# A four-layer attention kernel: one constant scale for all weights, and a first chunk in float16 parts

## Chip, core and metric

The kernel runs on one core of a Trainium2 chip. The metric is device time in microseconds (us) of one execution; lower is better. TensorE (PE) multiplies matrices, ScalarE (ACT) evaluates functions, VectorE (DVE) and GpSimd (POOL) do elementwise work, and SyncE (SP) issues the transfers (DMA) between the memory of the device (DRAM) and the memory beside the engines (SBUF). TensorE writes into PSUM, from which ScalarE and VectorE read.

## The reference

Four layers, windowed and full attention in turn, each with a layer norm before it and a residual addition behind it. S = 2048 rows, D = 512, H = 32 heads of 16, a window of 256 keys. Layers 0 and 2 use the A weights, layers 1 and 3 the B weights.

```python
def _A_ref(x, wqkv, wo):
    qkv = (x @ wqkv).reshape(B, S, 3, H, Dh).transpose(2, 0, 3, 1, 4)
    q, k, v = qkv[0], qkv[1], qkv[2]
    scores = jnp.einsum("bhqd,bhkd->bhqk", q, k) * (Dh ** -0.5)
    mask = (idx[:, None] - idx[None, :] >= 0) & (idx[:, None] - idx[None, :] < W)
    scores = jnp.where(mask[None, None], scores, -1e9)
    o = jnp.einsum("bhqk,bhkd->bhqd", softmax(scores), v)
    return o.transpose(0, 2, 1, 3).reshape(B, S, D) @ wo
# _B_ref: the same without the mask
x = x + _A_ref(_layernorm(x), A_wqkv, A_wo)
x = x + _B_ref(_layernorm(x), B_wqkv, B_wo)
x = x + _A_ref(_layernorm(x), A_wqkv, A_wo)
x = x + _B_ref(_layernorm(x), B_wqkv, B_wo)
```

The weights are drawn as 0.05 times standard normal numbers.

## The kernel before

**Tiling.** The rows are worked on in four chunks of 512 (`QC`, index `c`), the heads in eight groups of four (`qd`). `layers` and `mats` name eight weight matrices of 512 x 512, `(ty, s)`: `ty` is the kind of layer (0 windowed, 1 full), `s` is 0 for queries, 1 for keys, 2 for values, 3 for the output projection. For each chunk of a layer the kernel projects keys (`keys`, name `K`), queries (`queries`, `Q`) and values (`values`, `VV`), runs attention over the heads, and applies the output projection with the residual addition and the statistics of the next layer norm (`wo`, `OO`; in the last layer `wo_part`, `O3`, for a quarter of the heads at a time).

**Numbers in two float16 parts.** Activations and weights are split into a high part (the number rounded to float16) and a low part (what is left of it). A product is the sum of three matmuls, high by high, high by low and low by high (`TERMS`, line 439), so a projected tile of 128 x 512 takes 12 matmuls (four slices of the contraction). `mms` (line 419) emits them; in the full layers each is issued as four of 32 columns, one by one among the attention's matmuls.

**Scales.** So that the split holds for weights of any size, each column of a matrix is divided by a power of two near its largest magnitude. `maxima` (line 284) reduces the magnitudes on DVE and turns the result with four TensorE transposes; `scales` (line 312) cuts out the exponent, spreads it over the partitions with a product of a diagonal matrix and ones (`dg`, `ug`, L327), and puts the results in `wd`, `gcol` and `es`; `parts` (line 339) multiplies the matrix (`mul`, L344), casts it (ScalarE, L345) and subtracts (`rest`, L346), and writes the split matrix to DRAM (`wd`). `share` divides the exponents of queries and keys between both. What was divided out comes back where a result leaves PSUM: `es` in `project` (L525, L527, L528), `gcol` in `wo` and `wo_part` (L652, L673), each followed by an addition to x.

**The first chunk** is different. Its projections start before any scale is known, from unsplit float32 weights and a float32 copy `xT` of the normalized chunk, with four float32 matmuls a tile; the maxima are taken meanwhile (`first_maxima`), and the factors are applied when the tile leaves PSUM. The A matrices of queries, keys and values are split behind that (`parts(..., True)`) and stay in SBUF (`WT`) for the second chunk; all later users load them from DRAM (`weights`, line 391, L397 and L399). The other five matrices are prepared during the first layer's attention (`prep`, work `PR`).

**Order.** TensorE's order is written by hand: a planner with its own clock (`clock`, `spent`, `wait`) mixes "side" works (class `Work`: projections, output projections, preparations) with the attention's steps, three a group in the windowed layers and 16 a group in the full ones (`side0` to `side3` list them by chunk). A work marked `aside` costs TensorE little and is stepped on whenever its time has come. The instructions of all other engines, and SP's transfers, are put in order by a list scheduler from the program order, their dependencies and an estimate of durations; each engine then runs its own list strictly in order. A tile's `bufs` says how many buffers rotate under its tag: a load into a tag waits until the oldest buffer is free.

**Attention.** In the full layers a step is two pairs of score matmuls (L714), two exponentials of 128 x 1024 on ScalarE (L718) and four products with the values (L758); the side works there have one PSUM bank (`acc[1]`), which DVE empties. In the windowed layers POOL cuts the window out of the exponentials (L781, L784) before the products (L791). `epilogue` (line 678) turns the accumulated result on DVE (L686), divides it and splits it (`oh`, L701, L702).

The last lines compare the smallest and the sum of the softmax denominators with bounds and set `flag`; if it isn't good, `general_path` computes everything again.

Of the kernel before, what the change touches and what calls it, by code (L numbers as in the profile page):

```python
# [13 lines left out]
I32 = mybir.dt.int32  # L14
# [21 lines left out]
L_SUM = 2.0 ** 60  # L36

# [149 lines left out]
def fast_path(ctx, tc, flag, a_x, a_wqkv, a_wo, b_wqkv, b_wo, out):  # L187
# [21 lines left out]
    CM, DN, DC, WT, ST, pend = {}, {}, {}, {}, {}, []  # L209
# [16 lines left out]
    perm = cp.tile([P, P], F32, name="perm")  # L226
    onesf = cp.tile([P, P], F32, name="onesf")
    ones = cp.tile([P, QC], F16, name="ones")
    hsum = cp.tile([P, 32], BF16, name="hsum")
    es = cp.tile([P, 2, 2, NHT], F32, name="es")  # L230
    upv = cp.tile([P, 2, NHT], F32, name="upv")
    gcol = [cp.tile([P, D], F32, name=f"gcol{i}") for i in range(2)]
    zeros = cp.tile([P, QC], F16, name="zeros")
    lmin = cp.tile([P, QC // 32], F32, name="lmin")
    lsum = cp.tile([P, QC // 32], F32, name="lsum")

# [8 lines left out]
    nc.gpsimd.tensor_copy(perm.rearrange("p (h u d) -> p u h d", u=2, d=DH), ident.rearrange("p (u h d) -> p u h d", u=2, d=DH))  # L245
# [12 lines left out]
    nc.vector.memset(lsum, 0.0)  # L258

# [24 lines left out]
    def maxima(ty, s, raw):  # L284

        n = f"{ty}_{s}"
        if s == 3:
            for k in range(NC):
                nc.vector.tensor_scalar(raw[:, k, :], raw[:, k, :], upv[:, ty, k:k + 1], None, op0=ALU.mult)
        cm = CM[ty, s] = vp.tile([P, NHT], F32, name=f"wc{n}", tag="wc", bufs=8)  # L290
        am = vp.tile([P, D], F32, name=f"wa{n}", tag="dn", bufs=2)
        for h in range(4):
            f = slice(h * P, (h + 1) * P)
            nc.vector.tensor_reduce(am[:, f], raw[:, :, f].rearrange("p k f -> p f k"), axis=AX.X, op=ALU.max,
                                    apply_absolute_value=True)
            yield
        pt = bank().rearrange("p (t f) -> p t f", f=P)
        for t in range(NHT):
            nc.tensor.transpose(pt[:, t, :], am[:, t * P:(t + 1) * P], ident)
        nc.vector.tensor_reduce(cm, pt, axis=AX.X, op=ALU.max)  # L300

    def first_maxima(s, raw, tiles):

        if (0, s) not in CM:
            CM[0, s] = vp.tile([P, NHT], F32, name=f"wc0_{s}", tag="wc", bufs=8)
        for t in tiles:
            pt = bank()
            for k in range(NC):
                nc.tensor.transpose(pt[:, k * P:(k + 1) * P], raw[:, k, t * P:(t + 1) * P], ident)
            nc.vector.tensor_reduce(CM[0, s][:, t:t + 1], pt, axis=AX.X, op=ALU.max, apply_absolute_value=True)  # L310

    def scales(ty, s):

        n = f"{ty}_{s}"
        cm = CM.pop((ty, s))
        up = es[:, ty, s, :] if s < 2 else vp.tile([P, NHT], F32, name=f"wu{n}", tag="wc", bufs=8)
        dn = vp.tile([P, NHT], F32, name=f"wn{n}", tag="wc", bufs=8)
        nc.vector.tensor_scalar(up.bitcast(I32), cm.bitcast(I32), 0x7F800000, None, op0=ALU.bitwise_and)
        nc.vector.tensor_scalar(dn.bitcast(I32), up.bitcast(I32), -1, 0x7F000000, op0=ALU.mult, op1=ALU.add)
        DC[ty, s] = dn  # L320
        for v, name in ((up, "u"), (dn, "d"))[0 if s == 3 else 1:]:
            dg = vp.tile([P, NHT, P], F32, name=f"{name}g{n}", tag="oe")
            nc.vector.tensor_tensor(dg, ident[:, None, :].broadcast_to([P, NHT, P]),
                                    v[:, :, None].broadcast_to([P, NHT, P]), ALU.mult)
            yield
            pb = bank()
            nc.tensor.matmul(pb, onesf, dg.rearrange("p t f -> p (t f)"), start=True, stop=True)  # L327
            if name == "u":
                nc.vector.tensor_copy(gcol[ty], pb)
            else:  # L330
                DN[ty, s] = vp.tile([P, D], F32, name=f"wd{n}", tag="dn", bufs=2)
                nc.scalar.activation(DN[ty, s], pb, AF.Copy)
        if s == 2:

            pu = bank()
            nc.tensor.matmul(pu[:, :NHT], perm, up, start=True, stop=True)
            nc.vector.tensor_copy(upv[:, ty, :], pu[:, :NHT])

    def parts(ty, s, raw, act):

        dnb = DN.pop((ty, s))
        w = wp.tile([P, NC, 2, D], F16, name=f"w{ty}_{s}", tag="vf", bufs=NQ)
        hi, lo = w[:, :, 0, :], w[:, :, 1, :]
        mul = lambda k: (nc.vector if act else nc.gpsimd).tensor_tensor(raw[:, k, :], raw[:, k, :], dnb, ALU.mult)  # L344
        cast = lambda k: nc.scalar.activation(hi[:, k, :], raw[:, k, :], AF.Copy)  # L345
        rest = lambda k: nc.gpsimd.tensor_tensor(lo[:, k, :], raw[:, k, :], hi[:, k, :], ALU.subtract)  # L346
        if act:
            for k in range(NC):
                mul(k), cast(k), rest(k)
                yield  # L350
            WT[ty, s] = w
        else:

            for f, n, pause in (mul, 1, 2), (cast, 2, 1), (rest, 1, 0):
                for k in range(NC):
                    f(k)
                    if k % n == n - 1:
                        yield
                for _ in range(pause):
                    yield  # L360
        nc.sync.dma_start(wd[ty, s], w)

    def prep(ty, s):
        raw = load_w(ty, s)
        yield wait(14)
        for _ in maxima(ty, s, raw):
            yield wait(2)
        yield -spent(1.0)
        for _ in scales(ty, s):
            yield wait(4)  # L370
        if (ty, s) == (1, 0):
            share(1)
        yield -spent(0.5)
        for _ in parts(ty, s, raw, False):
            yield wait(2)

    def share(ty):

        s = vp.tile([P, NHT], F32, name=f"sh{ty}", tag="sh")
        h = vp.tile([P, NHT], F32, name=f"sg{ty}", tag="sh")  # L380
        q, k = (es[:, ty, i, :].bitcast(I32) for i in (0, 1))
        s, h = s.bitcast(I32), h.bitcast(I32)
        nc.vector.tensor_scalar(s, q, 1, None, op0=ALU.logical_shift_right)
        nc.vector.tensor_scalar(h, k, 1, None, op0=ALU.logical_shift_right)
        nc.vector.tensor_tensor(s, s, h, ALU.add)
        nc.vector.tensor_scalar(k, s, 0x7F800000, None, op0=ALU.bitwise_and)
        nc.vector.tensor_tensor(s, s, k, ALU.subtract)
        nc.vector.tensor_tensor(h, s, s, ALU.add)
        nc.vector.tensor_tensor(q, k, h, ALU.add)
# [103 lines left out]
    def transpose(l, c, xns):  # L493
        for i, xh in enumerate(xns):
            yield "wait", XNR[l, c] + 2.3 * i
            transposed(l, c, i, xh)

    def project(l, s, c, act, ht=None, first=None):


        ty, n = l % 2, f"{l}_{s}_{c}" + ("" if ht is None else f"_h{ht}")
# [540 lines left out]
    def all_of(works, following=()):  # L1042
        Side(1, works, following).finish()
# [151 lines left out]
```

## Time and profile before

| what | us |
| --- | --- |
| median of three runs | 2763.53 (2763.45 to 2769.7) |
| span of the profiled execution | 2769.2 |
| busy: PE | 2639.3 |
| busy: ACT | 2376.7 |
| busy: DVE | 961.8 |
| busy: POOL | 567.1 |
| first score matmul of the first layer (L714) | at 63.78 |

A row of the profile names line, engine and operation, then output and inputs by the program's names with their shapes and a count. Groups give busy time, the mean duration of one in ns, and the idle time of the engine ahead of them with what ended it. In an order-of-time view the first number is the start and the second the length; a bracket at the end is idle time ahead of the row and what ended it. "PEld" is the loading of TensorE's stationary operand, which overlaps matmuls. The chain and the waits are inferred from semaphores, and the ends of matmuls are modelled. Times are from one execution.

### The profile page before, as it was taken

The page shows a single profiled execution, that of the slowest core. Times are in us where ns is not written, and L with a number is a line of the kernel's source. Part 1 is how long each engine was busy: PE and PEld are TensorE (multiplying, and loading weights), DVE is VectorE, ACT ScalarE, POOL GpSimd, SP SyncE. Part 2 cuts the span into 40 slices and gives each one's busy share as a digit, 9 for nine tenths or more (in the row PEclk, how much of TensorE's full clock was granted, in tenths as well). Part 3 has the DMA queues.
Part 4 walks back from the last instruction along what each step waited for, and adds up shares of the span by engine and source line. Part 5 has one row for each costly group of instructions (what it writes and reads, how often), then busy time and mean ns, then how long its engine had stood idle before and what let it go on. Part 6 is the DMA issues. An engine that isn't in the chain of part 4 may idle for free.

```text
span 2769.2 us, 59663 instructions
## 1 busy us (share of the span) xinstructions
PE 2639.3 (95%) x24358; PEld 782.1 (28%) x24358; DVE 961.8 (35%) x2059; ACT 2376.7 (86%) x2687; POOL 567.1 (20%) x1129
## 2 busy tenths in 40 slices
PE   8989989999999999999998899899999999999997
PEld 4333334322222222222223333522222222222221
DVE  7678765112131113112215576512222222222122
ACT  3566655799999999999995667399999999999997
POOL 2477662000000000000004677200000000000000
PEclk9999999999999999999999999999999999999999
DMA  6877775422232123212325474613333343333331
GB/s 218 224 251 221 221 208 153 143 74 86 84 100 91 60 85 107 85 60 91 99 71 170 146 195 126 187 59 108 104 118 116 118 124 105 102 107 115 98 94 56
DMA packets 317501, 344.78 MB, mean 125 GB/s; under 512 B 113056, under 2 KB 233376, under 8 KB 311200
## 3 DMA queue, kind: packets, MB, share of 16 engines
q1 hardware_dynamic: 317216, 340.86, 40.3%
q8 instruction: 193, 3.16, 0.5%
q14 instruction: 92, 0.75, 0.1%
HBM read 228.07 MB, written 96.99 MB: 117 GB/s over the span
## 4 chain that ended last, share of the span: by engine, by line
PE 73%; ACT 9%; DVE 6%; issue 5%; POOL 3%; DMA 2%; SPq 0%; ACTq 0%; DVEq 0%; POOLq 0%
PE acc L758 30%; PE s L714 19%; PE b L432 10%; PE acc L429 10%; ACT e L718 8%; PE acc L791 3%; PE bs L432 1%; POOL e L781 1%; POOL e L784 1%; DVE ot L686 1%; POOL wr L344 1%; DVE sp L528 1%; DVE xh L469 0%; DVE xn L463 0%; DVE xh L463 0%
## 5 line engine op out<-in xcount | busy, mean ns | idle before, releaser
L718 ACT ACTIVATE e<-s 128x1024 f32<-128x1024 f32 (+2 forms) x2432 | 2243.3, 1116 | 99.4 <-PE s L714 89.4
L758 PE MATMUL acc<-e,vt 128*17 128x512 f32 x8192 | 1077.9, 598 | 5.3 <-DVE ot L686 4.1
L714 PE MATMUL s<-qt,kt 64*128 64x512 f16 (+3 forms) x5504 | 780.1, 355 | 64.7 <-ACT e L718 40.2
L714 PEld LDWEIGHTS <-kt 64*128 64x128 f16 x5504 | 204.6, 94 | 816.5 <-issue 789.8
L784 POOL TENSOR_SCALAR_AFFINE_SELECT e<-e 128x256 f32<-128x256 f32 x512 | 230.1, 457 | 119.2 <-ACT e L718 118.2
L758 PEld LDWEIGHTS acc<-e,vt 128*17 128x17 f32 x8192 | 136.2, 95 | 379.5 <-issue 347.9
L686 DVE STREAM_TRANSPOSE ot<-acc 128x512 f32<-128x512 f32 x128 | 91.3, 713 | 381.8 <-PE acc L758 317.3
L781 POOL TENSOR_SCALAR_AFFINE_SELECT e<-e 128x256 f32<-128x256 f32 x448 | 199.0, 451 | 92.2 <-ACT e L718 89.9
L702 POOL TENSOR_TENSOR oh<-o,oh 128x512 f16<-128x512 f32 x31 | 36.0, 1161 | 884.6 <-DVE oh L701 884.6
L791 PE MATMUL acc<-e,vt 128*17 128x384 f32 (+2 forms) x2816 | 204.2, 393 | 7.1 <-POOL e L781 4.8
L432 PE MATMUL b<-xc,w 128*128 128x512 f16 x684 | 162.5, 389 | 15.7 <-DVE sp L528 7.0
L533 POOL TENSOR_TENSOR sq_h<-sp_h 128x512 bf16<-128x512 f16 x27 | 28.1, 1040 | 484.0 <-DVE sp_h L527 484.0
L525 ACT ACTIVATE sp<-b,es 128x512 f16<-128x512 f32 x57 | 39.1, 687 | 98.1 <-PE b L432 95.9
L527 DVE TENSOR_SCALAR sp<-acc,es 128x512 f16<-128x512 f32 x28 | 20.9, 748 | 288.9 <-PE acc L429 288.9
L527 DVE TENSOR_SCALAR sp_h<-acc,es 128x512 f16<-128x512 f32 x27 | 20.3, 751 | 287.0 <-PE acc L429 287.0
L429 PE MATMUL acc<-xc,w_h 128*32 128x512 f16 x1296 | 108.6, 379 | 2.3 <-DVE km L566 2.3
L533 POOL TENSOR_TENSOR sq<-sp 128x512 bf16<-128x512 f16 x28 | 29.1, 1040 | 396.9 <-DVE sp L527 396.9
L429 PE MATMUL acc<-xc,w 128*32 128x512 f16 x1344 | 108.9, 379 | 0.3
L638 DVE COPY vt<-acc 128x256 f32<-128x256 f32 (+1 forms) x36 | 18.5, 513 | 257.6 <-PE acc L429 257.6
L673 DVE TENSOR_TENSOR dx<-acc,gcol 128x512 f32<-128x512 f32 x60 | 41.5, 692 | 176.6 <-PE acc L429 176.6
L429 PE MATMUL acc<-wo,oh 128*32 128x512 f16 x1296 | 101.3, 379 | 0.0
L432 PEld LDWEIGHTS <-w 128*128 128x128 f16 x720 | 68.1, 99 | 115.3 <-issue 37.5
(167 smaller groups left out, 1808.0 us busy)
## 6 DMA issues: line engine op xcount, KB each, us to landing
kt<-kf SPq DMA_DIRECT2D x128, 512.0 KB
qt<-qs SPq DMA_DIRECT2D x128, 256.0 KB
xd<-x SPq DMA_DIRECT2D x96, 256.0 KB
x<-xd SPq DMA_DIRECT2D x96, 256.0 KB
w<-wd SPq DMA_DIRECT2D x20, 1024.0 KB
kt<-kw SPq DMA_DIRECT2D x64, 256.0 KB
qs<-sp SPq DMA_DIRECT2D x48, 256.0 KB
wo<-wd SPq DMA_DIRECT2D x12, 1024.0 KB
```

What stands on the lines that cost most here:

```text
L429: nc.tensor.matmul(ps[g:g + 32], a[:, g:g + 32], b, start=(i == 0), stop=(i == len(pairs) - 1), skip_group_check=True)
L432: nc.tensor.matmul(ps, a, b, start=(i == 0), stop=(i == len(pairs) - 1))
L527: nc.vector.tensor_scalar(sp[:, 0], ps, e, None, op0=ALU.mult)
L533: nc.gpsimd.tensor_tensor(sq, sp[:, 0], sp[:, 0], ALU.mult)
L673: nc.vector.tensor_tensor(d, ps, gcol[1], ALU.mult)
L686: nc.vector.transpose(ot.rearrange("p b r -> p (b r)"), a)
L714: nc.tensor.matmul(ps[:, h, s0:s0 + wd_], kt[R * h:R * h + R, pr, kc:kc + P], qt[R * h:R * h + R, pr, qc:qc + wd_], start=True, stop=True)
L718: nc.scalar.activation(e[:, :, w0:w1], ps[:, :, w0:w1], AF.Exp, scale=SCALE)
L758: nc.tensor.matmul(a[32 * h:32 * h + DH + 1, :], V[l, qd // 4, j // 8][:, j % 8, 4 * (qd % 4) + h, :], es_[h // 2][:, h % 2, :], start=(j ...
L781: nc.gpsimd.affine_select(v, v, pattern=[[0, 2], [-1, P]], compare_op=ALU.is_gt, fill=0.0, base=0, channel_multiplier=1)
L784: nc.gpsimd.affine_select(v, v, pattern=[[0, 2], [1, P]], compare_op=ALU.is_ge, fill=0.0, base=0, channel_multiplier=-1)
L791: nc.tensor.matmul(a[32 * h:32 * h + DH + 1, q * P:(q + nb) * P], V[l, (4 * c + j) // 4][:, j % 4, 4 * qd + h, :], es_[h // 2][:, h % 2, s ...
```

## The change

All weights are multiplied by one constant, `WS` = 16, instead of a scale for each column. A matrix is split as soon as it is loaded: for each slice of the contraction ScalarE writes the high part `16 * w` as float16, and DVE writes the low part in one operation, `16 * w - high`. `maxima`, `first_maxima`, `scales`, `parts` and `share` are gone, and with them `perm`, `es`, `upv`, `gcol` and POOL's part in the preparation. Results are divided by 16 where they leave PSUM; in `wo` and `wo_part` that and the addition to x are one DVE operation, and the tile `d` is gone.

The first chunk is computed like the others: x and the first three matrices are split ahead of the projections, which use three float16 terms. The split matrices in SBUF are taken by the first chunk, so the second loads them from DRAM.

The order of the 12 matmuls in `project` and `values` is by term and then by slice, where it was by slice and then by term.

A new work `verify` (name `C`, `CW` in the list) reads each weight matrix once more in the first full layer, in four loads of 128 columns, takes the largest magnitudes of columns on DVE, and keeps their minimum and maximum in `wlow` and `whigh`. The last lines compare them with `W_MIN` and `W_MAX` beside the two old tests.

```diff
+WS = 16.0
+W_MIN, W_MAX = 2.0 ** -7, 4.0
...
+    def split(ty, s, raw):
+
+        w = wp.tile([P, NC, 2, D], F16, name=f"w{ty}_{s}", tag="vf", bufs=NQ)
+        for k in range(NC):
+            nc.scalar.activation(w[:, k, 0], raw[:, k], AF.Copy, scale=WS)
+            nc.vector.scalar_tensor_tensor(w[:, k, 1], raw[:, k], WS, w[:, k, 0], op0=ALU.mult, op1=ALU.subtract)
             yield
...
         nc.sync.dma_start(wd[ty, s], w)
+        return w
 
     def prep(ty, s):
         raw = load_w(ty, s)
         yield wait(14)
-        for _ in maxima(ty, s, raw):
+        yield -spent(0.5)
+        for _ in split(ty, s, raw):
             yield wait(2)
...
+    def verify(ty, s):
+
+        am = vp.tile([P, D], F32, name=f"wa{ty}_{s}", tag="wa", bufs=1)
+        for k in range(NC):
+            f = slice(k * P, (k + 1) * P)
+            raw = vp.tile([P, NC, P], F32, name=f"wc{ty}_{s}_{k}", tag="wc", bufs=2)
+            nc.sync.dma_start(raw, mats[ty, s][:, f].rearrange("(k p) f -> p k f", p=P))
+            yield wait(6)
+            nc.vector.tensor_reduce(am[:, f], raw.rearrange("p k f -> p f k"), axis=AX.X, op=ALU.max, apply_absolute_value=True)
+            yield wait(3)
+        at = vp.tile([P, D], F32, name=f"wt{ty}_{s}", tag="wc", bufs=2)
+        nc.vector.transpose(at, am)
+        mx = vp.tile([P, D // 32], F32, name=f"wx{ty}_{s}", tag="wx")
+        nc.vector.tensor_reduce(mx, at.rearrange("p (b r) -> p b r", r=32), axis=AX.X, op=ALU.max)
+        nc.vector.tensor_tensor(wlow, wlow, mx, ALU.min)
+        nc.vector.tensor_tensor(whigh, whigh, mx, ALU.max)
+        yield wait(3)
...
-                yield from mms(ps, [(w[:, k, a, w0:w0 + P], xc[:, b, k, :]) for k in range(NC) for a, b in TERMS], 2.2)
+            yield from mms(ps, [(w[:, k, a, w0:w0 + P], xc[:, b, k, :]) for a, b in TERMS for k in range(NC)], 2.2)
...
-                    nc.scalar.activation(sp[:, 0], ps, AF.Copy, scale=e)
+                    nc.scalar.activation(sp[:, 0], ps, AF.Copy, scale=1 / WS)
...
-            d = vp.tile([P, D], F32, name=f"dx{l}_{c}_{i}", tag="xn", bufs=1)
...
-                nc.vector.tensor_tensor(d, ps, gcol[l % 2], ALU.mult)
-            nc.vector.tensor_add(xs[i], xs[i], d)
+                nc.vector.scalar_tensor_tensor(xs[i], ps, 1 / WS, xs[i], op0=ALU.mult, op1=ALU.add)
...
-    xT = wp.tile([P, NC, QC], F32, name="xT", tag="xc", bufs=NQ)
-    first_maxima(1, raw[1], (0, 1))
+    xT = XC[0, 0] = wp.tile([P, 2, NC, QC], F16, name="xc0_0", tag="xc", bufs=NQ)
...
+    first_split(1)
     for i in range(4):
         nc.vector.tensor_scalar(xs[i], xs[i], mv[:, i, 0:1], y[:, i:i + 1], op0=ALU.subtract, op1=ALU.mult)
         pt = bank().rearrange("p (k n) -> p k n", n=P)
         for k in range(NC):
             nc.tensor.transpose(pt[:, k, :], xs[i][:, k * P:(k + 1) * P], ident)
-        nc.scalar.activation(xT[:, :, i * P:(i + 1) * P], pt, AF.Copy)
...
+        o = slice(i * P, (i + 1) * P)
+        nc.scalar.activation(xT[:, 0, :, o], pt, AF.Copy)
+        nc.vector.tensor_tensor(xT[:, 1, :, o], pt, xT[:, 0, :, o], ALU.subtract)
+    first_split(0)
+    run(keys(0, 0, True))
+    first_split(2)
+    run(queries(0, 0, True))
+    vals = values(0, 0, True)
...
     def side1():
-        a = [Q(1, c, False) for c in (2, 3)]
+        m = [(ty, s) for ty in range(2) for s in range(4)]
+        a = [CW(*x, [("C", *y)] if y else []) for y, x in zip([None] + m, m)]
+        a += [Q(1, c, False) for c in (2, 3)]
```

(`first_split(s)` runs `split(0, s, raw[s])` to its end and puts the tile in `WT`.)

199 lines of the change are left out of this document (43 added, 156 removed).

## The prediction

> **What bounds the kernel now.** I read the page first, then busy time by stretches, then the first 80 us in order of time, and then the waits and groups of the first layer.
>
> ```profile
> span 2769.2 us, 59663 instructions
> ...
> PE 2639.3 (95%) x24358; PEld 782.1 (28%) x24358; DVE 961.8 (35%) x2059; ACT 2376.7 (86%) x2687; POOL 567.1 (20%) x1129
> ...
> PE   8989989999999999999998899899999999999997
> ...
> POOL 2477662000000000000004677200000000000000
> ```
>
> TensorE is busy 95% of the span. POOL works only in two bands, slices 0 to 6 and 21 to 26: the two windowed layers. The full layers lie between, and there POOL is empty. Stretches of 50 us (PE, PEld, DVE, ACT, POOL busy us, then granted clock, DMA share, GB/s):
>
> ```profile
> 150.00:200.00 50.00, 43.67 (x380) 17.77 (x379) 37.85 (x73) 33.44 (x45) 38.31 (x74) 0.97 0.84 264
> ...
> 550.00:600.00 50.00, 50.00 (x644) 15.80 (x640) 5.45 (x14) 50.00 (x55) 1.16 (x1) 1.00 0.23 75
> ...
> 1650.00:1700.00 50.00, 45.14 (x499) 18.45 (x501) 28.94 (x64) 35.67 (x41) 38.31 (x97) 1.00 0.52 159
> ```
>
> In the full layer (550) ScalarE and TensorE are both busy 50.00 of 50, DVE 5.45. An edit on DVE or POOL gains nothing there; it can only disturb. In the first windowed layer (150) TensorE has 43.67 of 50, with DMA at 0.84, DVE and POOL at three quarters. So the gain has to come from TensorE's work and waits ahead of about 500 us.
>
> **Part A, the start (−13.6 us).** TensorE in order of time:
>
> ```profile
> 16.74 3.70 PE L432 MATMUL bs<-xT,wr 128*128 128x512 f32 x8 [0.20 <-DVE wc L310]
> 20.27 3.60 PE L432 MATMUL b<-xT,wr 128*128 128x512 f32 x8
> 23.71 3.60 PE L432 MATMUL bs<-xT,wr 128*128 128x512 f32 x8
> ...
> 30.57 1.02 PE L327 MATMUL bs<-dg,onesf 128*128 128x512 f32 x2
> ...
> 52.10 0.40 PE L550 MATMUL b<-sq,hsum 128*32 128x512 bf16 x4
> ...
> 63.78 0.50 PE L714 MATMUL s<-qt,kt 64*128 64x384 f16 x4
> ...
> 77.30 2.76 PE L432 MATMUL b<-xc,w 128*128 128x512 f16 x12
> 80.00 0.61 PE L714 MATMUL s<-qt,kt 64*128 64x384 f16 x8
> ```
>
> Between 16.74 and 63.78 TensorE hardly stops. A float32 projection tile takes 23.71 − 20.27 = 3.44 us, a tile of three float16 terms 80.00 − 77.30 = 2.70. The first chunk has 12 tiles: 41.3 us now, 32.4 after. Of the other 47.0 − 41.3 = 5.7 us (diagonal products as at 30.57, transposes for maxima, two head sums) only the two sums remain, like the L550 row, about 0.35 us each. The first tile can start when the normalized chunk is transposed and both it and the key weights are split. ScalarE gets four casts and four evictions, DVE four subtractions for weights, four normalizations and four subtractions for the chunk, some 7 us from 10.1. I let the first tile end at 19.7, as if it had begun at 17.0. The first score matmul then comes at 17.0 + 32.4 + 0.7 = 50.1: 63.78 − 50.1 = 13.7, taken as 13.6. If DVE normalizes first, 13.5 is the start and the gain 17. The other bound is the way of the queries to the attention:
>
> ```profile
> 55.18 0.74 DVE L582 TENSOR_SCALAR m_None<-b,kx 128x512 f16<-128x512 f32 x1
> ...
> 58.72 0.39 SPq L744 DMA_DIRECT2D qt<-qs  x1
> ```
>
> The shift row is done 3.4 us after the head sum of the queries (L550, ended 52.5), and the load of qt follows 2.8 us behind. After the change that sum ends near 42.0, so the load is issued near 48.3. At a landing of 2 us this ties with 50.1; at 6 us it costs 4, and the gain is 9.5.
>
> **Part B, later weights (−15 us).** Groups of 0 to 500 us (count | busy, mean ns of one | idle before):
>
> ```profile
> L346 POOL TENSOR_TENSOR w<-wr,w 128x512 f16<-128x512 f32 x32 | 40.5, 1290 | 49.2 <-ACT w L345 49.2
> ...
> L528 DVE SCALAR_TENSOR_TENSOR sp<-b,es,sp 128x512 f16<-128x512 f32 x45 | 33.3, 746 | 69.9 <-ACT sp L525 67.0 <-DMA wr<-in_A_wo_dram 2.9
> ...
> L344 POOL TENSOR_TENSOR wr<-wr,wd 128x512 f32<-128x512 f32 x20 | 27.4, 1394 | 1.4 <-ACT wd L332 1.3
> ...
> L469 DVE TENSOR_TENSOR xh<-xn,xh 128x512 f16<-128x512 f32 x28 | 20.6, 736 | 0.9 <-ACT xh L466 0.4
> ...
> L294 DVE TENSOR_REDUCE wa<-wr 128x128 f32<-128x512 f32 x20 | 20.4, 1071 | 2.3 <-DMA wr<-in_B_wqkv_dram 2.2
> ...
> L653 DVE TENSOR_TENSOR x<-x,dx 128x512 f32<-128x512 f32 x16 | 11.4, 713 | 0.5
> ...
> L327 PE MATMUL b<-dg,onesf 128*128 128x512 f32 x10 | 6.3, 720 | 1.8 <-DVE dg L323 1.8
> ...
> L299 PE MATMUL b<-ident,wa 128*128 128x128 f32 x20 | 3.3, 287 | 0.0
> ...
> L327 PE MATMUL b<-ug,onesf 128*128 128x512 f32 x4 | 2.3, 644 | 0.0
> ```
>
> Five matrices are prepared during the attention. TensorE loses the L299 transposes (3.3 us) and seven diagonal products of about 1.02 us a pair (the row at 30.57): 10.4 us. POOL loses 27.4 + 40.5 us. DVE gives up 20 reductions of 1.07 and gets 20 subtractions of two tensors: no row has this operation on SBUF data, and I cost it at the 0.736 of the two-tensor subtraction L469 (L528, of the same kind with one input in PSUM, has 0.746). ScalarE keeps its casts. Waits, 65 to 500 us (us in total, times, longest):
>
> ```profile
> PE s L714 <- ACT e L718: 13.6, 26, 1.5
> ...
> PE b L432 <- DVE sp L528: 7.0, 6, 2.4
> ...
> PE acc L791 <- POOL e L781: 4.8, 6, 1.4
> ...
> DVE st L449 <- DMA x<-in_A_x_dram: 3.9, 1, 3.9
> ```
>
> An engine that was never late gives nothing when relieved: POOL's 68 us are worth at most the 4.8 that TensorE idled for it, DVE's at most 7.0 plus the 1.8 for dg. I take 7.5 of the 10.4 (where side work vanishes, TensorE meets the 13.6 us of exponentials instead) and 7.5 of the 13.6 of waits: 15. Bounds: 5 and 24.
>
> The Trainium skill speaks against this step: its Vector Engine (DVE) Microarchitecture Reference, section 7, says that a scalar-tensor-tensor with two non-bf16 sources in SBUF runs at half throughput. By it each subtraction would take about 1.4 us instead of 0.74; no row here shows one, the nearest being L469 and L528. By the row the sum is 2740, by the rule 2747 (its own rival below).
>
> **Part C, transfers (+4 us).** Until now the chunk after the first found its three split matrices in SBUF; now the first chunk uses them up and the second loads 3 x 1 MB again, each like this row of the page:
>
> ```profile
> w<-wd SPq DMA_DIRECT2D x20, 1024.0 KB
> ```
>
> DMA from 0 to 64 and from 64 to 200 us (packets, MB, share of 16 engines):
>
> ```profile
> q1 hardware_dynamic: 12560, 13.37, 64.7%
> ...
> q1 hardware_dynamic: 29688, 32.47, 81.1%
> ```
>
> 32.47 MB in 136 us are 239 GB/s; 3 MB more are 12.5 us if nothing is free, and a shorter start packs the rest closer. With 19% to 35% free I charge a third: 4; bounds 0 and 12.5.
>
> **Part D, the check (+5 us).** 32 loads of 256 KB, 32 reductions like L294 (34 us of DVE) and 8 short ends are programmed into the first full layer, where DVE has 5.45 of 50. But the queues other than TensorE's do not keep program order when something is ready early:
>
> ```profile
> 203.90 0.46 SPq L266 DMA_DIRECT2D kf<-ones x1
> ...
> 258.04 0.49 DVE L701 CAST oh<-o 128x512 f16<-128x512 f32 x1
> ...
> PEld acc L758 <- DVE ot L686: 17.3, 31, 1.8
> ```
>
> The fill of kf belongs behind the eighth output cast (258.04), and SP issues it at 203.90. A check load depends on nothing but its two buffers, so I expect many of them, with their reductions, in the last 100 us of the windowed layer, where DVE is used and a late load holds everything behind it on DVE: evictions, which TensorE waits for. In the full layer the transposition L686 is what waits behind; the 17.3 us are its present price. The 20 reductions and evictions of the old preparation met 2.2 + 2.9 = 5.1 us of late loads, 0.26 each; for 32 that is 8.3, and I let 5 arrive at TensorE. Bounds: 0, and 32 x (1.07 + 0.26) = 43.
>
> **Part E, additions (−4.2 us).** The product with gcol and the addition (L653, 0.71) become one operation on the PSUM data. It lies on the path where a layer ends (0.65 saved at two layer ends: 1.3), eases DVE in the third layer (1), and at the end:
>
> ```profile
> 2758.43 1.49 PE L432 MATMUL b<-wo,oh 128*128 128x512 f16 x3
> ...
> 2761.92 0.69 DVE L674 TENSOR_TENSOR x<-x,dx 128x512 f32<-128x512 f32 x1
> ```
>
> The last product ends at 2759.92, the last addition at 2762.61; one operation of 0.75 ends at 2760.7: 1.9 us. In the full layers it is hidden behind ScalarE's exponentials. Bounds: 0 and 8. The order of the terms (all of one kind over k, then the next) changes no count of matmuls or weight loads; I give it nothing beside the start, where high parts can begin first.
>
> **Sum.** −13.6 − 15 + 4 + 5 − 4.2 = −23.8. The profiled execution goes from 2769.2 to 2745.4; it is the slowest of the three runs (2769.7), 5.7 over their median of 2763.53, so I predict 2740.
>
> **Rivals.**
> 1. The forecast, 2728 to 2752: chance 0.58.
> 2. The transfers set the pace: for it, DMA at 81% up to 200 us; against, 35% free in the first 64. Then C is 12.5 and B only 5: −13.6 − 5 + 12.5 + 5 − 4.2 = −5.3, 2758. Chance 0.14.
> 3. The check's reductions stand at DVE's head waiting for loads, in the windowed layer's last stretch and at L686: −28.8 + 43 = +14, 2777. It makes the kernel slower from 37 us, 1.16 us for each of the 32. For it, the single wait of 3.9 us for x; against, DMA at 0.23 in the full layer. Chance 0.12.
> 4. All waits of B fall away (24) and C and D are free: −13.6 − 24 − 4.2 = −41.8, 2722. Chance 0.08.
> 5. Slow subtractions: doubled from 0.736, four ahead of the first tile cost 2.9, and the evictions behind the others keep their waits (4 us of B lost): 2747. Chance 0.06. (This is the case of the Trainium skill's rule above.)
> 6. A column falls outside the bounds and the general path runs behind: 4 x 32 x 16 rows of 2048 exponentials, each two of L718's 1.1 us, are 4.5 ms more, some 7.2 ms.
>
> ```profile
> L718 ACT ACTIVATE e<-s 128x1024 f32<-128x1024 f32 (+2 forms) x2432 | 2243.3, 1116 | 99.4 <-PE s L714 89.4
> ```
>
> Columns of 0.05 noise have maxima far within 2^-7 and 4. Chance 0.02.
>
> A measurement tells 0.3% (8.3 us) from no change. Faster than 2755 are 1, 4, 5 and a little of 2: 0.76. Within are most of 2 and the edge of 1: 0.11. Slower are 3 and 6: 0.13. The range from 2722 to 2768 leaves out 6, most of 3 and the lower edge of 4.
>
> **What would show it.** A: the first L714 row near 50 instead of 63.78. B: no POOL work beside selections before 500 us, and the full layer's first matmuls (L758) some 25 us earlier. C: waits of TensorE for w, xc or kt in the first 130 us. D: where the new reductions start, their DMA waits on DVE, and the length of the first full layer, which should keep its length within 3 us. E: one DVE row after the last product. I am wrong if the first full layer starts less than 12 us earlier, or if it becomes longer by more than 10.

## The result, and the profile after

The changed kernel takes 2773.41 us (median of 15 runs, 2769.67 to 2776.54), the kernel before 2766.17 us beside it (15 runs, 2760.83 to 2771.91). The ratio is 1.0029, with a 95% interval of 1.0021 to 1.0037: slower by about 7 us, where 24 us less were forecast. The profiled execution went from 2769.2 to 2771.7.

The page of the changed kernel: span, busy times, and the slices of TensorE and POOL.

```profile
span 2771.7 us, 59403 instructions
...
PE 2616.8 (94%) x24314; PEld 767.5 (28%) x24314; DVE 852.9 (31%) x1949; ACT 2365.6 (85%) x2683; POOL 492.8 (18%) x1074
...
PE   7888988999999999999998889899999999999998
...
POOL 1445542000100000000004577200000000000000
```

Every engine has less work: PE 22.5 us, DVE 108.9, ACT 11.1, POOL 74.3. The time grew all the same, so TensorE waits more: in the first seven slices, the first windowed layer, its digits read 7888988 where they read 8989989 before.

To see where, I cut that layer at the output casts (DVE, one for each quarter of a chunk's heads; every fourth ends a chunk's attention). Each row is start, length, engine, line, operation. Those of the first, third and fourth chunk before (the second is in the prediction, 258.04):

```profile
163.87 0.62 DVE L701 CAST oh<-o 128x512 f16<-128x512 f32 x1
...
358.89 0.53 DVE L701 CAST oh<-o 128x512 f16<-128x512 f32 x1
...
455.22 0.43 DVE L701 CAST oh<-o 128x512 f16<-128x512 f32 x1
```

The same in the changed kernel, all four (line numbers moved by 87 there):

```profile
147.46 0.40 DVE L614 CAST oh<-o 128x512 f16<-128x512 f32 x1
...
252.74 0.43 DVE L614 CAST oh<-o 128x512 f16<-128x512 f32 x1
...
346.65 0.43 DVE L614 CAST oh<-o 128x512 f16<-128x512 f32 x1
...
461.51 0.42 DVE L614 CAST oh<-o 128x512 f16<-128x512 f32 x1
```

With the first score matmul and the first and last products of the full layers (first seen 512.7 and last 2750.8 before, 516.6 and 2755.8 after; the third layer, a windowed one, lies between them) this gives the lengths in us. Each column is one execution; runs of one kernel lie 2 to 11 us apart, so a difference of 1 or 2 us in one row says little. The last column is the first experiment below, the changed kernel without its check.

| stretch | before | after | without the check |
| --- | --- | --- | --- |
| to the first score matmul | 63.8 | 52.6 | 54.0 |
| first chunk | 100.1 | 94.8 | 94.3 |
| second chunk | 94.2 | 105.3 | 105.4 |
| third chunk | 100.9 | 93.9 | 93.9 |
| fourth chunk | 96.3 | 114.9 | 94.9 |
| to the first full layer | 57.5 | 55.1 | 57.0 |
| first to last product of the full layers | 2238.1 | 2239.2 | 2239.7 |
| to the end | 18.4 | 15.9 | 17.1 |

The lead over before was 11.2 us at the first scores and 16.4 after the first chunk. The second chunk gave back 11, the third won 7 again, and the fourth lost 18.6. From the first full layer on little differs. That layer begins 3.9 us later than before. So there are two losses to explain, in the second and in the fourth chunk.

The fourth chunk has the check in it. The changed kernel's rows of the tile `wc` (count, then shortest, median and longest duration in ns, first and last start, and VectorE's idle time ahead of them with the number of waits):

```profile
L310 DVE TENSOR_REDUCE wa<-wc x32: 976/1045/1099, 355.7 to 467.2; 128x128 f32<-128x512 f32 x32
L308 SPq DMA_DIRECT2D wc<-in_A_wqkv_dram x12: 367/398/1257, 351.4 to 387.1; - x12
...
  DMA wc<-in_B_wqkv_dram: 10.8, 8
  DMA wc<-in_A_wqkv_dram: 8.7, 7
  DMA wc<-in_A_wo_dram: 2.5, 2
  DMA wc<-in_B_wo_dram: 1.3, 2
```

The work is programmed into the first full layer, which begins at 516.6; all 32 reductions ran some 50 to 160 us ahead of it, as the prediction expected of many of them, and VectorE stood 23.3 us in front of them waiting for loads. TensorE's waits in that stretch, 345 to 470 us (total, times, longest):

```profile
PE b L361 <- DMA w<-wd: 8.1, 1, 8.1
PE bs L361 <- DVE oh L614: 5.9, 1, 5.9
PE b L361 <- DVE x L569: 3.0, 2, 2.7
```

Two of the three are waits for VectorE. The wait for `w` was there before too (6.6 us in the same stretch); the other two were not, and the kernel without the check has no wait of TensorE for VectorE there at all.

In the second chunk TensorE shows these rows (start, length, and in the bracket the idle time ahead with its cause):

```profile
165.58 4.27 PE L361 MATMUL b<-xc,w 128*128 128x512 f16 x12 [2.87 <-DVE km L490]
...
194.54 1.03 PE L627 MATMUL s<-qt,kt 64*128 64x128 f16 x8 [5.52 <-DMA kt<-kw]
...
218.45 0.62 PE L704 MATMUL acc<-e,vt 128*17 128x128 f32 x4 [3.39 <-POOL e L694]
```

And SP's queue shortly before the second of them:

```profile
186.93 0.57 SPq L660 DMA_DIRECT2D kt<-kw  x1
187.55 7.27 SPq L281 DMA_DIRECT2D wr<-in_B_wo_dram  x8
```

The keys that TensorE lacks until 194.54 are issued just ahead of the eight loads of B's output matrix. Before, those eight stood between 270 and 308 us, in the third chunk. That the load moved forward is measured, and so are the loads of the three matrices prepared ahead of it: 117 to 172 us, where it was 119 to 185. The reason is read from the code and no wait of the trace shows it: splitting a matrix takes two short operations instead of a long chain, so its buffer (`vf`) comes free earlier.

The reload itself lies elsewhere. Its three transfers are issued at 44.07, 55.05 and 85.28 us (SP's queue, L326), at the start and in the first chunk, and that is where TensorE waits beside them: 3.53 us for the first queries and, in the row below, 6.04 for keys, where the kernel before had 1.67.

```profile
103.64 0.82 PE L627 MATMUL s<-qt,kt 64*128 64x384 f16 x4 [6.04 <-DMA kt<-kw]
```

### The profile page after: what moved, and what is told of

Read it like the earlier page. It is cut to its first block, busy times and chain, and to the rows that moved or that the text cites. A ratio compares the mean times of both kernels' runs of the same rounds, so it can differ in the third digit from the quotient of the medians.

```text
span 2771.7 us, 59403 instructions
## 1 busy us (share of the span) xinstructions
PE 2616.8 (94%) x24314; PEld 767.5 (28%) x24314; DVE 852.9 (31%) x1949; ACT 2365.6 (85%) x2683; POOL 492.8 (18%) x1074
## 4 chain that ended last, share of the span: by engine, by line
PE 72%; ACT 10%; DVE 5%; issue 5%; DMA 4%; POOL 2%; SPq 1%; ACTq 0%; DVEq 0%
PE acc L671 30%; PE s L627 19%; PE acc L358 9%; ACT e L631 9%; PE b L361 9%; PE acc L704 3%; PE bs L361 2%; POOL e L694 1%; POOL e L697 1%; DVE ot L599 1%; DMA wc<-in_A_wqkv_dram 1%; DMA wc<-in_B_wqkv_dram 1%; DMA qt<-qs 1%; DVE wa L310 1%; DMA kt<-kw 0%
## 5 line engine op out<-in xcount | busy, mean ns | idle before, releaser
L697 POOL TENSOR_SCALAR_AFFINE_SELECT e<-e 128x256 f32<-128x256 f32 x512 | 224.2, 444 | 196.5 <-ACT e L631 195.3
L694 POOL TENSOR_SCALAR_AFFINE_SELECT e<-e 128x256 f32<-128x256 f32 x448 | 198.4, 449 | 124.1 <-ACT e L631 122.4
L449 ACT ACTIVATE sp<-b 128x512 f16<-128x512 f32 x58 | 34.7, 598 | 108.8 <-PE b L361 98.2
L361 PEld LDWEIGHTS <-w 128*128 128x128 f16 x816 | 77.2, 100 | 126.2 <-issue 36.6
L451 DVE TENSOR_SCALAR sp_h<-acc 128x512 f16<-128x512 f32 x27 | 18.6, 690 | 287.1 <-PE acc L358 287.1
L587 DVE SCALAR_TENSOR_TENSOR x<-acc,x 128x512 f32<-128x512 f32 x60 | 41.5, 692 | 206.1 <-PE acc L358 199.8
L451 DVE TENSOR_SCALAR sp<-acc 128x512 f16<-128x512 f32 x28 | 19.3, 689 | 263.4 <-PE acc L358 262.1
L556 DVE TENSOR_SCALAR vt<-acc 128x256 f32<-128x256 f32 (+1 forms) x36 | 18.5, 513 | 257.8 <-PE acc L358 257.8
```

The costliest lines, as they stand in the source:

```text
L361: nc.tensor.matmul(ps, a, b, start=(i == 0), stop=(i == len(pairs) - 1))
L451: nc.vector.tensor_scalar(sp[:, 0], ps, 1 / WS, None, op0=ALU.mult)
L587: nc.vector.scalar_tensor_tensor(xs[i], ps, 1 / WS, xs[i], op0=ALU.mult, op1=ALU.add)
L694: nc.gpsimd.affine_select(v, v, pattern=[[0, 2], [-1, P]], compare_op=ALU.is_gt, fill=0.0, base=0, channel_multiplier=1)
L697: nc.gpsimd.affine_select(v, v, pattern=[[0, 2], [1, P]], compare_op=ALU.is_ge, fill=0.0, base=0, channel_multiplier=-1)
```

## The experiments

Two theories were set against each other first. Theory 1: the check, hoisted out of the full layer, costs what is missing. Theory 2: the transfers do, the reload of 3 MB and the closer packing. The check alone in the kernel before, for which 12 to 20 us more were expected, gave no time: its tiles leave 34.2 KB per partition of SBUF where the pool `probs` needs 40. So what the check costs is known only on top of the other parts.

**The check left out** (the eight `CW` works are gone, so no column is checked):

```diff
-        a = [CW(*x, [("C", *y)] if y else []) for y, x in zip([None] + m, m)]
-        a += [Q(1, c, False) for c in (2, 3)]
+        a = [Q(1, c, False) for c in (2, 3)]
```

> The changed kernel without the eight verify works: the weights' magnitudes are not checked. Theory 1 (the check's loads and reductions, moved by the scheduler into 355 to 468 us, delay the last chunk of the first layer; its lead over the old kernel goes there from 12.2 us to a lag of 3.1): the time falls by 15 to 19 us from 2773, to about 2756, ratio 0.996 to the kernel before, and the first full layer starts near 497. Theory 2 (what was won at the start is lost to the three added 1 MB loads and the closer packed transfers, and the check is hidden): within 4 us of 2773. Theory 3 (the other order of terms or the new split costs all along): within 4 us of 2773.

Measured: 2758.08 us (2754.83 to 2759.18), ratio to before 0.9963, interval 0.9949 to 0.9976. 15.3 us less than with the check. The fourth chunk is 20.0 us shorter, and the start, the way to the full layer and the end are 1 to 2 us longer each. The fourth chunk's attention ends here:

```profile
442.56 0.43 DVE L614 CAST oh<-o 128x512 f16<-128x512 f32 x1
```

instead of at 461.51. The second chunk stays long (105.4), so theory 1 explains one loss and not the other.

**The check held where it is programmed.** A copy of `lmin`, which the attention keeps changing, into the buffer gives each load something to wait for:

```diff
             raw = vp.tile([P, NC, P], F32, name=f"wc{ty}_{s}_{k}", tag="wc", bufs=2)
+            nc.vector.tensor_copy(raw[:, 0, :QC // 32], lmin)
             nc.sync.dma_start(raw, mats[ty, s][:, f].rearrange("(k p) f -> p k f", p=P))
```

> The changed kernel with a copy of 16 numbers of lmin into each check tile ahead of its load, so that the load cannot start before the step of the full layer where it was programmed. Nothing is left out. Theory 1: the check costs nothing in the full layer, and the time is that of the kernel without the check within 3 us, about 2756. A rival (34 us of DVE and 8 MB cost the same wherever they stand, since DVE empties the only bank of the side work there): no gain, 2770 or more, with the full layer 10 us or more longer.

Measured: 2756.55 us (2755.87 to 2759.17), ratio 0.9961, interval 0.9946 to 0.9975. The reductions now run inside the full layer:

```profile
L311 DVE TENSOR_REDUCE wa<-wc x32: 1033/1067/1107, 595.2 to 955.2; 128x128 f32<-128x512 f32 x32
```

The same loads and reductions, and the same time as without them: first to last product 2240.0 against 2239.7. In the full layer the check costs next to nothing: that layer takes 952.5 us against 949.8 without the check (951.2 to 952.5 in the five kernels that hold the check there, 948.1 to 949.8 in the six others). Its price is one of place.

**The first three split matrices kept**, so the second chunk doesn't load them again (the check stays hoisted):

```diff
-            return WT.pop((ty, s))
+            return WT[ty, s] if n in ("0_1_0", "0_0_0", "v0_0_0_0") else WT.pop((ty, s))
```

> The changed kernel with the three split A matrices kept in SBUF until the second chunk has used them, as in the old kernel, so that the 3 MB of added loads fall away; the check stays where it is. Theory 2: the 11 us that the lead loses between 147 and 253 us come back, about 2762. Theory 1: the lead is greater at 250 us, but most of the end stays, 2766 to 2773.

Measured: 2764.4 us (2760.44 to 2767.66), ratio 0.9988, interval 0.9978 to 0.9998. That is 9.0 less than the change, between theory 2's 2762 and theory 1's 2766 to 2773. The first scores no longer wait:

```profile
50.32 0.50 PE L627 MATMUL s<-qt,kt 64*128 64x384 f16 x4
```

But the 11 us of the second chunk, which theory 2 gave to the reload, did not come back. That chunk still takes 102.8 us, and its wait for keys is longer than in the change (5.52):

```profile
193.82 1.03 PE L627 MATMUL s<-qt,kt 64*128 64x128 f16 x8 [7.28 <-DMA kt<-kw]
```

So the reload costs something, and it is not what fills the second chunk.

**Kept, with the check held**, the two edits above together:

> The kernel with the check held back to the full layer and the three split A matrices kept for the second chunk. If the two costs add: 2756.5 minus the 9 us that keeping gave beside the check in its place, 2748. If the gain of keeping was partly that of the disturbed end: 2751 to 2754.

Measured: 2749.59 us (2748.77 to 2751.01), ratio 0.9944, interval 0.9927 to 0.9961: 7.0 less than with the check held alone. Of the 8.2 us between the two profiled executions 3.7 are at the first scores (53.86 to 50.12) and 4.5 in the second chunk (106.5 to 102.0), whose wait for keys stays (6.2 after 7.6). The time lies between the two that were set against each other, nearer to the sum.

**B's output matrix prepared one chunk later**, with the check held. The preparation moves from one list of side works to the next, and its load gets the same kind of copy to wait for:

```diff
+        if (ty, s) == (1, 3):
+            nc.vector.tensor_copy(raw[:, :, :QC // 32], lmin[:, None, :].broadcast_to([P, NC, QC // 32]))
...
-            return [..., PR(1, 2, [("P", 1, 1)]), T(1, 0), PR(1, 3, [("P", 1, 0)])]
+            return [..., PR(1, 2, [("P", 1, 1)]), T(1, 0)]
...
-            return [..., VV(0, 3), K(1, 0), T(1, 1)]
+            return [..., VV(0, 3), K(1, 0), T(1, 1), PR(1, 3, [("P", 1, 0)])]
```

> The kernel with the check held back to the full layer, and the last weight preparation (the output projection of the full layer: eight loads of 128 KB, split, store) moved from chunk 1 to chunk 2 and held there by a copy of lmin into its tile. Theory C (transfers packed into 150 to 220 us, these eight loads among them, make the wait of 6.9 us for kt at 195 and the lowered clock behind it): chunk 1 becomes 7 to 10 us shorter than its 106.5, and the time is 2747 to 2751. Rival (kt is late for another reason, the transposing transfers or the 3 MB of added loads): the wait stays or moves, and the time is within 3 us of 2756.5.

Measured: 2746.37 us (2743.44 to 2748.14), ratio 0.9933, interval 0.9916 to 0.995. 10.2 less than with the check held alone. The wait for keys that was 7.64 in that kernel is now

```profile
194.00 0.61 PE L630 MATMUL s<-qt,kt 64*128 64x128 f16 x8 [2.40 <-DMA kt<-kw]
```

and the second chunk takes 91.8 us instead of 106.5, more than the 7 to 10 us that were expected; the third chunk, to which the preparation went, takes 2.8 us more. Busy time from 150 to 250 us (PE, PEld, DVE, ACT, POOL, then granted clock, DMA share, GB/s), first of the change, then of this run:

```profile
150.00:250.00 100.00, 80.89 (x705) 31.63 (x705) 56.15 (x133) 55.40 (x71) 50.66 (x123) 0.90 0.85 241
```

```profile
150.00:250.00 100.00, 89.01 (x816) 36.11 (x813) 61.85 (x148) 63.06 (x81) 58.79 (x138) 0.98 0.93 255
```

More is transferred here, and TensorE still gets 8 us more work done at a higher granted clock. So bytes alone were not the trouble. What is shown is that this preparation in this place cost some 10 us; that it was its loads beside the keys fits the wait, which is 5.2 us shorter, but its four casts, four subtractions and its store moved with them and were not tried apart.

**The check's work taken away, its loads left.** Where the check stands in the change, the reductions read 8 of each 128 columns, and the transpose and last reduction shrink with them (so only a sixteenth of the columns is checked). The transposed tile also leaves the two buffers of the loads for its own. This asks by what the check costs in the fourth chunk: by its late loads, as the prediction had it, or by VectorE's own work.

```diff
-            nc.vector.tensor_reduce(am[:, f], raw.rearrange("p k f -> p f k"), ...)
+            nc.vector.tensor_reduce(am[:, 8 * k:8 * k + 8], raw[:, :, :8].rearrange("p k f -> p f k"), ...)
```

> The changed kernel with the check at its place, with the same loads, but reductions over 8 of each 128 columns and a short end: 120 of 128 columns are not looked at. DVE's work for the check falls from about 50 us to a few, its waits for the loads stay. If DVE's standing still for late loads decides (the theory of the prediction): the loss stays, 2768 to 2774. If DVE's own work in that stretch decides: 2758 to 2762.

Measured: 2760.09 us (2755.48 to 2761.99), ratio 0.9979, interval 0.9968 to 0.9991: 13.3 of the 15.3 us are gone. The reductions of 340 to 470 us (count, busy, mean ns, idle before and its causes):

```profile
L310 DVE TENSOR_REDUCE wa<-wc 128x8 f32<-128x32 f32 x32 | 6.5, 205 | 32.4 <-DMA wc<-in_A_wqkv_dram 14.6 <-DMA wc<-in_B_wqkv_dram 13.7 <-DMA wc<-in_B_wo_dram 4.1
```

VectorE stood longer for loads than in the change (32.4 against 23.3 us), and the kernel was faster.

**The loads taken away, the work left**, the counterpart: only the first 128 columns of each matrix are loaded, and all four reductions read them.

```diff
-            raw = vp.tile([P, NC, P], F32, name=f"wc{ty}_{s}_{k}", tag="wc", bufs=2)
-            nc.sync.dma_start(raw, mats[ty, s][:, f].rearrange("(k p) f -> p k f", p=P))
+            if k == 0:
+                raw = vp.tile([P, NC, P], F32, name=f"wc{ty}_{s}_{k}", tag="wc", bufs=2)
+                nc.sync.dma_start(raw, mats[ty, s][:, f].rearrange("(k p) f -> p k f", p=P))
```

> Each weight matrix of the check is loaded for its first 128 columns only (8 loads of 256 KB in place of 32), and the four reductions a matrix all read that tile: the reductions stay 32 of the same size, a quarter of the loads is left. So only a part of the columns is checked. This is the counterpart of the run with the thin reductions. If VectorE's own work in the last stretch of the windowed layer is what costs, the time stays near that of the change: 2767 to 2773, the fourth chunk 110 us or longer. If the late loads cost (the step of the prediction), most of the 15 us goes: 2757 to 2762, the fourth chunk near 97 us, as without the check.

Measured: 2771.33 us (2766.14 to 2772.38), ratio 1.0015, interval 1.0006 to 1.0024: 2.1 less than the change, whose interval it meets. The fourth chunk takes 109.7 us, 5.2 less than in the change; the start took 2.5 more.

```profile
L311 DVE TENSOR_REDUCE wa<-wc 128x128 f32<-128x512 f32 x32 | 32.0, 1035 | 6.1 <-DMA wc<-in_A_wqkv_dram 3.3 <-DMA wc<-in_B_wqkv_dram 2.5 <-DMA wc<-in_B_wo_dram 0.3
```

Three quarters of the waiting for loads is gone and nearly all of the cost is still there. 13.3 and 2.1 together are the 15.3 of the whole check; in the fourth chunk alone they are 13.7 and 5.2 of 20.0. What both runs do in the stretch of 340 to 470 us, in the order change, without the check, thin reductions, one load:

```profile
340.00:470.00 130.00, 107.01 (x922) 48.05 (x920) 95.69 (x186) 60.08 (x79) 52.46 (x131) 0.92 0.70 206
```

```profile
340.00:470.00 130.00, 121.54 (x1038) 57.31 (x1029) 67.81 (x156) 68.72 (x94) 53.99 (x134) 0.97 0.58 172
```

```profile
340.00:470.00 130.00, 116.89 (x1029) 55.50 (x1026) 73.71 (x223) 67.59 (x91) 54.63 (x137) 0.96 0.77 232
```

```profile
340.00:470.00 130.00, 109.62 (x959) 49.30 (x952) 98.00 (x200) 62.83 (x82) 55.19 (x138) 0.93 0.56 166
```

TensorE's busy time is low in the two rows where VectorE's (the third engine of a row) is high, and doesn't follow the DMA share (0.70, 0.58, 0.77, 0.56). The two runs differ from the change in the order of VectorE's queue as well as in its work, since the list scheduler places shorter work elsewhere; how much of the 13 us is the work and how much its order was not separated.

**The old order of terms** (slice by slice), with the check held:

```diff
-[... for a, b in TERMS for k in range(NC)]
+[... for k in range(NC) for a, b in TERMS]
```

> The kernel with the check held back to the full layer and the old order of the 12 matmuls (by slice, then by term). Theory: the order matters only for the first tile, within 2 us of 2756.5. Rival (the order costs in all projections): 4 us or more away from it.

Measured: 2758.45 us (2754.66 to 2763.21), ratio 0.9975, interval 0.9965 to 0.9984. That is 1.9 us more than with the check held alone, and the intervals meet, so no gain of the new order is clear of the noise. The first scores come at 56.07 instead of 53.86; behind them nothing is longer that would speak for a cost in all projections, as the prediction had it.

**All three edits together**: the check held, the matrices kept, B's output matrix later.

> Three edits together: the check held back into the full layer, the first three split matrices kept in SBUF for the second chunk, and the preparation of B's output matrix one chunk later. Against the version with the check held back (2756.6), keeping gave -7.0 and the later preparation -10.2. If both relieve different places they add up: 2739 to 2741, ratio near 0.991 to the kernel before. If both take the same stall from the second chunk (their transfers stood in the same 70 us), little is added to the larger: 2745 to 2748.

Measured: 2742.51 us (2740.12 to 2743.66), ratio 0.9919, interval 0.9905 to 0.9932. That is the fastest of all, 23 us under the kernel before. It missed the additive 2739 to 2741 by 1.5 us: of 7.0 + 10.2, 14.0 came; that the two edits share some 3 us of one stall is likely and not shown. Its check on VectorE, from 577 to 940 us:

```profile
L313 DVE TENSOR_REDUCE wa<-wc 128x128 f32<-128x512 f32 x32 | 33.7, 1068 | 39.3 <-DMA wc<-in_A_wqkv_dram 16.4 <-DMA wc<-in_B_wqkv_dram 14.9 <-DMA wc<-in_B_wo_dram 5.0
```

VectorE waits longer for these loads than in the change (39.3 against 23.3 us; 41.3 with the check held alone), and there it has the time.

## Why the prediction was wrong

By its own terms, in us of the profiled executions (A to C from the kernel without the check, D from the change against it):

| term | forecast | measured | from |
| --- | --- | --- | --- |
| A, start | −13.6 | −9.8 | first scores 63.8 to 54.0 |
| B, later weights | −15 | −14.5 | first, third and fourth chunk and the way to the full layer: −5.7, −6.9, −1.4, −0.5 |
| C, transfers | +4 | +11.3 | second chunk |
| D, check | +5 | +15.3 | with and without it |
| E, additions | −4.2 | +0.3 | first full layer to the end: +1.6, then −1.3 |
| sum | −23.8 | +2.6 | profiled: +2.5 |

**The step that failed is D, and C was mis-sized.** D put a price on late loads alone and none on VectorE's own work. C priced the reload and not the load that moves forward into the second chunk. Together they are 17.6 us over the forecast, which is two thirds of the miss; A and E make up nearly all of the rest. The prediction's own sign says the same: the first full layer was to start some 25 us earlier, and at least 12, and it starts 3.9 us later, while its length stays (949.3 after 949.4), as forecast.

**A** was right in its mechanism, and its other bound is what came. TensorE of the changed kernel:

```profile
15.53 4.20 PE L361 MATMUL bs<-xc,w 128*128 128x512 f16 x12 [1.66 <-ACT xc L989]
19.57 2.75 PE L361 MATMUL b<-xc,w 128*128 128x512 f16 x12
...
46.34 2.75 PE L361 MATMUL b<-w,xc 128*128 128x512 f16 x12
...
52.62 0.82 PE L627 MATMUL s<-qt,kt 64*128 64x384 f16 x4 [3.53 <-DMA qt<-qs]
```

The first tile ends at 19.7 as forecast (it begins earlier and takes longer), the last at 49.1, one us ahead of the 50.1 forecast for the scores, and then TensorE waits 3.53 us for the queries. The prediction named this load as the other bound (issued near 48.3, a gain of 9.5 for a landing of 6 us). It took the tie, and the reload of C broke it: with the three matrices kept the first scores came at 50.12 and 50.32, the forecast to 0.2 us. A and C were costed apart, though both use the same queue in the same 10 us.

**B** comes to 14.5 for 15 on the stretches outside the second chunk, and that is in part luck. Almost half of it, 6.9, is the third chunk, from which the preparation of B's output matrix has gone into the second. With all three edits, where that preparation stands in the third chunk again, the third chunk takes 101.6 us and the way from the first scores to the first full layer 438.4 instead of 448.9: there B is worth 10.6. Which waits it takes away is less sure still: those for exponentials are 13.3 us after and were 13.6 before, those for POOL's selections 4.1 after 4.8.

**C** was charged with a third of the reload's 12.5 us. The reload cost 7.0 (kept, check held), of which 3.7 fell at the start, and its waits lie in the first 130 us, where the prediction looked for them. The 11.3 of the table are something else: they are lost in the second chunk, where no reload runs. What the step left out is that the other weight loads move too. The prediction saw that POOL's 68 us go from the preparation and asked only what TensorE gains by that; it did not ask which transfers then come earlier, and beside which urgent one. Moving that one preparation back gave 10.2. Rival 2 (transfers set the pace) had 12.5 for C, near the 11.3, but for the reload, so that is luck; its B of 5 was too small.

**D** was right in that the check leaves the full layer and lands in the last 100 us of the windowed one, and right that it costs little in the full layer (some 2 us). The price was worked out from late loads: 32 waits of 0.26 us, of which 5 us arrive. The loads were later than that, 23.3 us instead of 8.3, but three quarters of them carry only about 2 us of the price (5.2 of 20.0 in the fourth chunk), about the 5 that the forecast allowed. The other 13 come and go with VectorE's own work, 33.4 us of reductions and 11 of transposes and last reductions, which the sum gave no price at all: it stood only in the upper bound of 43. Whether by its length or by the order that it forces on VectorE's queue stays open. What mattered was VectorE's busy time in the stretch where the work would land, not where it was programmed: without the check VectorE has 67.81 of 130 us there, some 44 us were put on top, and its evictions and output casts are what TensorE's next matmuls need (the 5.9 us for `oh` above). Rival 3 had the place and the sign, with a price for work and waits together (37 us were to decide; 15 of 43 came, and that was enough only because C cost more and A and E gave less as well).

**E** saved 2.5 us at the end, where 1.9 were forecast. One row is left after the last product, as forecast:

```profile
2763.15 0.81 PE L361 MATMUL bs<-wo,oh 128*128 128x512 f16 x3
```

```profile
2764.00 0.69 DVE L587 SCALAR_TENSOR_TENSOR x<-bs,x 128x512 f32<-128x512 f32 x1
```

The 2.3 us expected at layer ends and in the third layer do not show: the third layer (277.1 before, 273.3 to 277.9 in the ten changed kernels) and the whole from first to last product (2238.1 before, 2234.7 to 2240.1) lie on both sides of the value before. What does show is 1.1 us in the last full layer, 947.9 or 948.0 in all ten after 949.1, where the prediction called the saving hidden; which edit gives it was not tried.

**Rival 5**, the slow subtraction, is refuted. The split of a whole matrix, and the group of all 32 over the first 500 us in the kernel without the check:

```profile
216.14 2.49 DVE L290 SCALAR_TENSOR_TENSOR w<-wr,w 128x512 f16<-128x512 f32 x4
```

```profile
L290 DVE SCALAR_TENSOR_TENSOR w<-wr,w 128x512 f16<-128x512 f32 x32 | 20.7, 684 | 4.6 <-ACT w L289 4.6
...
L398 DVE TENSOR_TENSOR xh<-xn,xh 128x512 f16<-128x512 f32 x28 | 19.7, 703 | 0.9 <-ACT xh L395 0.4
```

684 ns with two SBUF sources, a float32 and a float16 one, against 703 for the plain subtraction of the same size. The rule of the Trainium skill (Vector Engine (DVE) Microarchitecture Reference, section 7) doesn't hold for this form here.

The forecast without C and D would be 2769.2 − 13.6 − 15 − 4.2 = 2736.4. The version with all three edits, which still does the whole check, has a span of 2738.4, in the fastest of its five runs. By terms that is A −14.2, B −10.6 and E −6.0, so the sum fits better than its parts. A gain near the one forecast is there; the change as made gives it back in two places.

## What to carry to other kernels

When a preparation becomes shorter, the loads behind it can move forward: list them, and look which urgent load they then stand beside. Work without dependencies doesn't stay where it is programmed; cost it in the stretch where a scheduler can put it, with its whole busy time there, or give it a dependency that holds it in a stretch where its engine is idle. The chain of waits names what ended last, and that is not the price: take the work and the wait away one at a time.

## What the runs showed beyond that

**The chain blamed the loads.** Pieces of the changed kernel's chain of waits in the fourth chunk (start, length, what):

```profile
353.02 4.35 DMA wc<-in_A_wqkv_dram
...
359.45 4.77 DMA wc<-in_A_wqkv_dram
...
367.57 4.16 DMA wc<-in_A_wqkv_dram
371.75 1.08 DVE wa L310
```

From 340 to 462 us the check's loads had 36% of the chain (16.9, 15.9 and 3.2), its first reductions 14.1%. By the two counterpart runs it is 2.1 us for three quarters of the loads and 13.3 for most of the work.

**A short stall is paid again in the clock.** TensorE in the run with one load for each matrix of the check, and the granted clock of the changed kernel in 10 us around a stall and in the 10 us after it (the number behind POOL's):

```profile
374.14 5.28 PE L362 MATMUL b<-wo,oh 128*128 128x512 f16 x12 [2.41 <-DVE x L570]
...
381.15 2.76 PE L362 MATMUL b<-wo,oh 128*128 128x512 f16 x12
```

```profile
190.00:200.00 10.00, 5.46 (x32) 1.90 (x33) 2.21 (x5) 1.94 (x2) 2.21 (x6) 0.66 1.09 150
200.00:210.00 10.00, 8.64 (x90) 3.49 (x88) 8.60 (x28) 6.57 (x10) 4.59 (x11) 1.00 0.48 171
```

After 2.41 us without work the same 12 matmuls took 5.28 us instead of 2.76: the stall cost 2.5 us more than its length. The granted clock is 0.50 from 374.0 to 379.5 us, and by the trace's record it fell at 373.1, 1.4 us after the last product. The Trainium skill (TensorE: Matmul & The Clock Gate, Part 1) says that TensorE runs at half clock after an idle window of about 3.4 us until it has been busy as long; the halved rate agrees, and here an idle time shorter than that window was enough. No wait in the prediction was charged with this. From 50 to 520 us the clock was at half for 27 us before, 58 in the change, 48 without the check and 27 with all three edits. TensorE worked in 22 of the 27 us and in 37 of the 58; if that work would take half the time at full clock, as the 12 matmuls nearly do, the 15 us more are a loss of 7 to 8 us, which is an estimate.
